# Linear attention and a gated FFN on one core: attention per whole batch on full 128x128 products, remainder tokens pooled in a ninth block, Gelu on ScalarE, loads cast on GpSimd, a fixed order

## The chip, the cores and the metric

One Trainium2 chip, one of its eight cores. The metric is the device time of one execution in microseconds; lower is better. Engines: TensorE (PE), VectorE (DVE), ScalarE (ACT), GpSimd (POOL) and SyncE (SP), the last only as a queue that issues DMAs. A tile lies in SBUF, or in PSUM, where TensorE writes its products.

## What is computed

Attention of a linear kind (softmax over the head dimension for q, over the tokens for k), whose output, laid out as tokens by channels, goes through a gated FFN. Eight batches, 8 heads, 576 tokens, 64 channels per head, all inputs float32.

```python
def _attn_ref(q, k, v):                          # (8, 8, 576, 64) each
    q_s = np.exp(q - max(q, axis=-1)); q_s = q_s / sum(q_s, axis=-1)
    k_s = np.exp(k - max(k, axis=2));  k_s = k_s / sum(k_s, axis=2)
    kv = np.einsum('bhsd,bhse->bhde', k_s, v)
    return np.einsum('bhsd,bhde->bhse', q_s, kv)

def _moe_ref(x, w_gate, w_val, w_out):           # x (4608, 512), weights 512x1536, 512x1536, 1536x512
    g = x @ w_gate
    gelu = 0.5 * g * (1.0 + erf(g / sqrt(2)))
    return (gelu * (x @ w_val)) @ w_out
```

Both kernels leave out the subtraction of the maxima, and divide kv by the column sums of exp(k), which a column of ones beside v provides.

## The kernel before

Two parts share the engines. **Attention** works on pairs of heads, 32 units (8 batches x 4 pairs). A pair's 1152 tokens lie on 128 partitions as nine chunks of 128, so chunk 4 holds the last 64 tokens of one head and the first 64 of the other. `attention_load` (lines 84 to 105) loads q and k by SP in runs of 256 B (one token's 64 floats) and v by a GpSimd DMA that casts to f16. `attention_main` (lines 107 to 168) takes exp on ACT, normalizes q on DVE (L115 sum, L117 reciprocal, L119 product), transposes q by ten TensorE products per pair (L128 to L137, copied to SBUF by ACT, L140 and L141), forms kv in ten small products (`pskv_a`, `pskv_b`, 65 columns, L145 to L153), and scales the two results into a block-diagonal 128x128 tile on DVE (L157 to L165). `attention_out` (lines 170 to 180) makes the pair's 128 channels of x for 576 tokens with two products (L174 of 512 columns, L176 of 64), cast by ACT into `xt_sb`, which holds x transposed for all 4608 tokens.

**The FFN** (`ffn_block`, lines 182 to 229) goes over nine blocks of 512 tokens, in order of token, so a block crosses batches. In each of 12 steps `fi` it forms 128 columns of gate (`psg`, four products, L191) and value (`psv`, L196), and the gated f16 tile `ht`: tanh on ACT (L200, Gelu as 0.5 g (1 + tanh)), then three passes on DVE (L204, L207, L210). Then four groups `psy` of 12 products each (L219) give 128 tokens of output; ACT scales them (L223) and SP stores them.

Before block 0 stand batch 0's attention, the loads of batch 1 and the issue of the gate and value weights (GpSimd DMAs that cast, 128 columns each). `ffn_block` then runs one attention stage (a load, a `main` or an `out` of batch blk+1 or blk+2) ahead of each `fi` step. The program's order is only the start: a scheduler at build time sets the order on each engine by its own costs, and pools of buffers (three of each attention tile, four PSUM banks for `psg`, `psv`, `psy` and `psxa`) limit how far it runs ahead.

Of the kernel before, what the change touches and what calls it, by code (L numbers as in the profile page):

```python
# [10 lines left out]
f16 = mybir.dt.float16  # L11

_TANH_C = 0.7978845608028654
# [4 lines left out]
def kernel(  # L18
# [13 lines left out]
    NTOK = B * S  # L32
# [3 lines left out]
    NCH = (2 * S) // P  # L36
    NCI = C // P
    NFI = F // P
    NBLK = 512
    NB = NTOK // NBLK  # L40
# [3 lines left out]
    xpool = ctx.enter_context(tc.tile_pool(name="xpool", bufs=1))  # L44
    att = ctx.enter_context(tc.tile_pool(name="att", bufs=3))
    ffn = ctx.enter_context(tc.tile_pool(name="ffn", bufs=3))
    htp = ctx.enter_context(tc.tile_pool(name="htp", bufs=24))
    ps_big = ctx.enter_context(tc.tile_pool(name="ps_big", bufs=4, space=bass.MemoryType.PSUM))
    ps_eqt = ctx.enter_context(tc.tile_pool(name="ps_eqt", bufs=2, space=bass.MemoryType.PSUM))
    ps_kv = ctx.enter_context(tc.tile_pool(name="ps_kv", bufs=2, space=bass.MemoryType.PSUM))  # L50

    def big_psum(name):
        return ps_big.tile([P, 512], f32, name=name, tag="mm")

    def small_psum(name):
        return ps_kv.tile([P, 72], f32, name=name, tag="kv")

    ident = const.tile([P, P], f16)
    make_identity(nc, ident)

    xt_sb = xpool.tile([P, H // 2, NTOK], f16)

    wtiles = {}

    def load_weights_gv():
        wg_sb = wpool.tile([P, NCI, F], f16, name="wg_sb")
        wv_sb = wpool.tile([P, NCI, F], f16, name="wv_sb")
        wg_src = moe_w_gate.rearrange("(ci p) f -> p ci f", p=P)
        wv_src = moe_w_val.rearrange("(ci p) f -> p ci f", p=P)
        for fi in range(NFI):  # L70
            sl = slice(fi * P, (fi + 1) * P)
            nc.gpsimd.dma_start(out=wg_sb[:, :, sl], in_=wg_src[:, :, sl])
            nc.gpsimd.dma_start(out=wv_sb[:, :, sl], in_=wv_src[:, :, sl])
        wtiles["g"] = wg_sb
        wtiles["v"] = wv_sb

    def load_weights_o():
        wo_sb = wpool.tile([P, NFI, C], f16, name="wo_sb")
        wo_src = moe_w_out.rearrange("(fi p) m -> p fi m", p=P)
        for fi in range(NFI):  # L80
            nc.gpsimd.dma_start(out=wo_sb[:, fi, :], in_=wo_src[:, fi, :])
        wtiles["o"] = wo_sb

    def attention_load(b: int, hp: int):
        h0 = 2 * hp
        qt = att.tile([P, NCH, D], f32)
        nc.sync.dma_start(
            out=qt,
            in_=q[b, h0:h0 + 2].rearrange("h s d -> (h s) d").rearrange(
                "(n p) d -> p n d", p=P),  # L90
        )
        kt = att.tile([P, NCH, D], f32)
        nc.sync.dma_start(
            out=kt,
            in_=k[b, h0:h0 + 2].rearrange("h s d -> (h s) d").rearrange(
                "(n p) d -> p n d", p=P),
        )
        vt = att.tile([P, NCH, 80], f16)
        nc.gpsimd.dma_start(  # L99
            out=vt[:, :, 0:D],  # L100
            in_=v[b, h0:h0 + 2].rearrange("h s d -> (h s) d").rearrange(
                "(n p) d -> p n d", p=P),
        )
        nc.vector.memset(vt[:, :, D:D + 1], 1.0)
        return qt, kt, vt

    def attention_main(b: int, hp: int, tiles):
        qt, kt, vt = tiles
        eq = att.tile([P, NCH, D], f16)
        nc.scalar.activation(out=eq, in_=qt, func=mybir.ActivationFunctionType.Exp)  # L110
        ek = att.tile([P, NCH, D], f16)
# [70 lines left out]
    def ffn_block(blk: int, interleave=()):  # L182
# [45 lines left out]
        for fn in inter:  # L228
            fn()
# [67 lines left out]
```

## Time and profile before

| | |
|---|---|
| median of 3 runs | 383.56 us (383.49 to 384.02) |
| the profiled execution, from first to last instruction | 381.9 us |
| PE busy | 350.7 us, 92% of the span, 2000 matmuls |
| DVE busy | 275.4 us, 72% |
| ACT busy | 187.6 us, 49% |
| POOL busy | 57.0 us, 15% |
| DMA | 38.10 MB, 131739 packets, of which 125568 under 512 B |
| mean granted TensorE clock | 0.973 of full speed |

The times are of unprofiled runs; the profile is one more execution, whose own time is known by its span. In the profile a group of instructions is a line of the kernel with its engine; in the groups the columns after the bar are the busy time in us, the mean of one in ns, then the engine's idle time just before them and what ended most of it. The chain of work that ended last lists start, length and work of each piece. The slices cut the span into 40 equal parts with the busy share in tenths.

### The profile page before, as it was taken

The page shows a single profiled execution, that of the slowest core. Times are in us where ns is not written, and L with a number is a line of the kernel's source. Part 1 is how long each engine was busy: PE and PEld are TensorE (multiplying, and loading weights), DVE is VectorE, ACT ScalarE, POOL GpSimd, SP SyncE. Part 2 cuts the span into 40 slices and gives each one's busy share as a digit, 9 for nine tenths or more (in the row PEclk, how much of TensorE's full clock was granted, in tenths as well). Part 3 has the DMA queues.
Part 4 walks back from the last instruction along what each step waited for, and adds up shares of the span by engine and source line. Part 5 has one row for each costly group of instructions (what it writes and reads, how often), then busy time and mean ns, then how long its engine had stood idle before and what let it go on. Part 6 is the DMA issues. An engine that isn't in the chain of part 4 may idle for free.

```text
span 381.9 us, 5586 instructions
## 1 busy us (share of the span) xinstructions
PE 350.7 (92%) x2000; PEld 167.7 (44%) x2000; DVE 275.4 (72%) x612; ACT 187.6 (49%) x337; POOL 57.0 (15%) x74
## 2 busy tenths in 40 slices
PE   2698582899999999999999999999999999999995
PEld 1444231345444544454445444545455444444442
DVE  3558275387986799679967987698568927954980
ACT  3764523537663757375737563657166313323321
POOL 5574444202010102010202020102010000000000
PEclk9999696699999999999999999999999999999999
DMA  9999999996685459546953883454130011011002
GB/s 164 202 194 169 168 173 184 194 237 112 100 94 145 74 78 124 146 66 88 120 149 65 120 94 100 71 65 31 66 62 2 0 67 45 0 46 66 0 1 110
DMA packets 131739, 38.10 MB, mean 100 GB/s; under 512 B 125568, under 2 KB 127104, under 8 KB 131712
## 3 DMA queue, kind: packets, MB, share of 16 engines
q1 hardware_dynamic: 79936, 28.32, 34.3%
q0 software_dynamic: 51776, 9.44, 29.8%
q8 instruction: 15, 0.25, 0.3%
q14 instruction: 12, 0.10, 0.1%
HBM read 37.75 MB, written 9.44 MB: 124 GB/s over the span
## 4 chain that ended last, share of the span: by engine, by line
PE 78%; DMA 14%; DVE 4%; ACT 2%; issue 1%; SPq 1%; ACTq 0%; DVEq 0%
PE psy L219 24%; PE psg L191 22%; PE psv L196 21%; DMA kt<-in_k_dram 9%; DMA qt<-in_q_dram 5%; PE pseqt_a L133 2%; PE pseqt_b L137 2%; DVE gv L207 2%; PE psxa L174 2%; PE pskv_b L153 1%; DVE gsc L204 1%; DVE ht L210 1%; PE pseqt_a L128 1%; PE pskv_a L147 1%; PE pskv_a L145 1%
## 5 line engine op out<-in xcount | busy, mean ns | idle before, releaser
L196 PE MATMUL psv<-xt_sb,wv_sb 128*128 128x512 f16 x432 | 113.3, 385 | 6.6 <-ACT xt_sb L179 5.7
L204 DVE TENSOR_SCALAR gsc<-psg 128x512 f32<-128x512 f32 x108 | 74.1, 687 | 62.5 <-ACT tnh L200 60.9
L191 PE MATMUL psg<-xt_sb,wg_sb 128*128 128x512 f16 x432 | 115.9, 389 | 0.0
L219 PE MATMUL psy<-wo_sb,ht 128*128 128x512 f16 x432 | 94.9, 379 | 0.2 <-DVE ht L210 0.2
L200 ACT ACTIVATE tnh<-psg 128x512 f32<-128x512 f32 x108 | 64.0, 594 | 58.8 <-PE psg L191 44.7
L207 DVE TENSOR_TENSOR gv<-gsc,psv 128x512 f32<-128x512 f32 x108 | 73.1, 678 | 4.0 <-PE psxb L176 1.6
L210 DVE SCALAR_TENSOR_TENSOR ht<-tnh,gv 128x512 f16<-128x512 f32 x108 | 73.3, 681 | 0.5
L196 PEld LDWEIGHTS <-wv_sb 128*128 128x128 f16 x432 | 42.7, 99 | 60.0 <-issue 10.0
L219 PEld LDWEIGHTS <-ht 128*128 128x128 f16 x432 | 41.9, 98 | 51.7 <-DVE ht L210 3.1
L99 POOL DMA_DIRECT2D vt<-in_v_dram x32 | 32.0, 1001 | 203.8 <-PE pskv_b L153 85.2
L191 PEld LDWEIGHTS <-wg_sb 128*128 128x128 f16 x432 | 38.5, 99 | 45.2 <-issue 3.9
L223 ACT ACTIVATE yo<-psy 128x512 f32<-128x512 f32 x36 | 21.5, 597 | 67.3 <-PE psy L219 67.3
L112 ACT ACTIVATE ek<-kt 128x576 f16<-128x576 f32 x32 | 21.9, 683 | 20.1 <-DMA kt<-in_k_dram 19.0
L110 ACT ACTIVATE eq<-qt 128x576 f16<-128x576 f32 x32 | 21.7, 679 | 18.4 <-DMA qt<-in_q_dram 9.4
L119 DVE TENSOR_TENSOR eqn<-eq,rrq 128x576 f16<-128x576 f16 x32 | 24.0, 750 | 5.8 <-PE pseqt_b L137 5.6
L140 ACT COPY eqt_sb<-pseqt_a 64x576 f16<-64x576 f16 x32 | 20.2, 630 | 14.9 <-PE pseqt_a L128 14.3
L115 DVE TENSOR_REDUCE rq<-eq 128x9 f32<-128x576 f16 x32 | 23.0, 722 | 6.0 <-ACT eq L110 5.9
L179 ACT CAST xt_sb<-psxa 128x512 f16<-128x512 f32 x32 | 18.7, 584 | 10.1 <-PE psxb L176 10.0
L174 PE MATMUL psxa<-eqt_sb,kv_sb 128*128 128x512 f16 x32 | 13.6, 426 | 10.1 <-ACT eqt_sb L141 8.8
L141 ACT COPY eqt_sb<-pseqt_b 64x576 f16<-64x576 f16 x32 | 20.2, 631 | 0.9
L133 PE MATMUL pseqt_a<-ident,eqn 128*64 128x128 f16 x128 | 15.1, 239 | 3.1 <-ACT eqt_sb L140 2.3
L145 PE MATMUL pskv_a<-vt,ek 128*64 128x65 f16 x128 | 10.3, 203 | 7.2 <-DMA vt<-in_v_dram 7.0
(35 smaller groups left out, 184.9 us busy)
## 6 DMA issues: line engine op xcount, KB each, us to landing
qt<-in_q_dram SPq DMA_DIRECT2D x32, 288.0 KB, 4.8
kt<-in_k_dram SPq DMA_DIRECT2D x32, 288.0 KB, 4.9
out_dram<-yo SPq DMA_DIRECT2D x36, 256.0 KB, 2.0
vt<-in_v_dram POOLq DMA_DIRECT2D x32, 144.0 KB, 5.1
wg_sb<-in_moe_w_gate_dram POOLq DMA_DIRECT2D x12, 128.0 KB, 12.1
wv_sb<-in_moe_w_val_dram POOLq DMA_DIRECT2D x12, 128.0 KB, 12.2
wo_sb<-in_moe_w_out_dram POOLq DMA_DIRECT2D x12, 128.0 KB, 9.2
```

Of the source, the lines that this page charges most:

```text
L99: nc.gpsimd.dma_start(out=vt[:, :, 0:D], in_=v[b, h0:h0 + 2].rearrange("h s d -> (h s) d").rearrange("(n p) d -> p n d", p=P),)
L112: nc.scalar.activation(out=ek, in_=kt, func=mybir.ActivationFunctionType.Exp)
L115: nc.vector.reduce_sum(rq, eq, axis=mybir.AxisListType.X)
L119: nc.vector.tensor_tensor(out=eqn, in0=eq, in1=rrq.unsqueeze(-1).to_broadcast((P, NCH, D)), op=mybir.AluOpType.mult,)
L133: nc.tensor.transpose(pseqt_a[0:64, j * P:(j + 1) * P], eqn[:, j, :], ident[:, :])
L191: nc.tensor.matmul(psg, wtiles["g"][:, ci, fi * P:(fi + 1) * P], xt_sb[:, ci, t0:t0 + NBLK], start=(ci == 0), stop=(ci == NCI - 1))
L196: nc.tensor.matmul(psv, wtiles["v"][:, ci, fi * P:(fi + 1) * P], xt_sb[:, ci, t0:t0 + NBLK], start=(ci == 0), stop=(ci == NCI - 1))
L200: nc.scalar.activation(out=tnh, in_=psg, func=mybir.ActivationFunctionType.Tanh, scale=_TANH_C)
L204: nc.vector.tensor_scalar(out=gsc, in0=psg, scalar1=0.5 * _H_SCALE, scalar2=None, op0=mybir.AluOpType.mult)
L207: nc.vector.tensor_tensor(out=gv, in0=gsc, in1=psv, op=mybir.AluOpType.mult)
L210: nc.vector.scalar_tensor_tensor(out=ht, in0=tnh, scalar=1.0, in1=gv, op0=mybir.AluOpType.add, op1=mybir.AluOpType.mult)
L219: nc.tensor.matmul(psy, hts[fi][:, ns * P:(ns + 1) * P], wtiles["o"][:, fi, :], start=(fi == 0), stop=(fi == NFI - 1))
```

## The change

The kernel is written anew around one batch at a time; the arithmetic of the FFN stays in products of 128x128 by 512 columns, nine blocks of 512 columns.

- **Blocks.** Of each batch's 576 tokens, 512 (on 128 partitions, four consecutive tokens each) are FFN block b. The other 64 of each batch are collected in `xtr` (8 x 64 = 512 columns), which is a ninth block at the end.
- **Attention.** A pair of heads is the 128 columns of one weight load. kv takes five products of 130 columns per pair (`unit_kv`, the fifth for the 64 remainder tokens, padded with zeros), whose off-diagonal halves a mask removes in the scaling. Transposes are full 128x128, four per pair and one for the remainder (`unit_t`, `unit_trem`). x is one product of 512 columns per pair (`unit_x`) and one of 64 (`unit_xrem`). The normalization of q runs on four heads at a time (`norm_sum`, `norm_mul`).
- **Engines.** Gelu is one ACT pass, and `ht` one DVE pass (value x 1024 x gelu). Transposed q is copied by DVE; x is copied by DVE up to batch 2 and by ACT from batch 3; DVE scales the output.
- **Loads.** All are plain float32 DMAs of SP: q, k and v in runs of 1 KB (remainder 256 B), weights in runs of 2 KB, 1 MB each, into eight shared staging buffers (`ldp`). GpSimd casts v and all weights to f16.
- **Order.** `manual_schedule` keeps each engine's instructions as written. Batch 1 and 2 get their norms and most of their attention behind the last output groups of blocks 0 and 1; batches 3 to 7 inside the steps of blocks 2 to 6.

Where things stand is read from the order of instructions on an engine. The first place is DVE at the passage from block 1 to block 2. Before (`rq`, `rrq`, `eqn`: norms of later pairs; `gsc`: the first pass of block 2's first step):

```order
L210 SCALAR_TENSOR_TENSOR ht_1857<-tnh_1851,gv_1855 128x512
L119 TENSOR_TENSOR eqn_2044<-eq_2036,rrq_2042 128x576
L161 MEMSET kv2_sb_2077 128x64
L115 TENSOR_REDUCE rq_2201<-eq_2197 128x9
L161 MEMSET kv2_sb_2238 128x64
L117 RECIPROCAL rrq_2203<-rq_2201 128x9
L115 TENSOR_REDUCE rq_2264<-eq_2260 128x9
L119 TENSOR_TENSOR eqn_2205<-eq_2197,rrq_2203 128x576
L117 RECIPROCAL rrq_2266<-rq_2264 128x9
```

Now (`yo`: scaled output of block 1; `rq`, `rrq`, `eq0`: norms of batch 2; `eqt`, `xt`: copies of its transposed q and of its x, which block 2's first products read):

```order
L159 TENSOR_REDUCE rq_879<-eq0_97 128x20
L163 RECIPROCAL rrq_881<-rq_879 128x20
L169 TENSOR_TENSOR eq0_97<-eq0_97,rrq_881 128x5x256
L267 TENSOR_SCALAR yo_877<-psy_884 128x512
L208 COPY eqt_899<-pst_900 128x2x512
L208 COPY eqt_899<-pst_910 128x2x512
L216 COPY eqt_899<-pstr_920 128x4x64
L229 CAST xt_926<-psx_927 128x512
L229 CAST xt_926<-psx_930 128x512
L229 CAST xt_926<-psx_933 128x512
L229 CAST xt_926<-psx_936 128x512
L253 SCALAR_TENSOR_TENSOR ht_969<-psv_962,gl_967 128x512
```

Before, DVE works there for later pairs, since block 2's x was finished inside block 1; now norms and copies of the very batch that block 2 reads stand between the blocks.

The second place is ACT between the same blocks. Before:

```order
L200 ACTIVATE tnh_1339<-psg_1329 128x512
L110 ACTIVATE eq_1973<-qt_1411 128x576
L223 ACTIVATE yo_1360<-psy_1347 128x512
L223 ACTIVATE yo_1376<-psy_1363 128x512
L110 ACTIVATE eq_2036<-qt_1436 128x576
L223 ACTIVATE yo_1392<-psy_1379 128x512
L223 ACTIVATE yo_1408<-psy_1395 128x512
L200 ACTIVATE tnh_1428<-psg_1418 128x512
```

Now (a table load, then the Exp of batch 2, `ek0` and `eq0`, and of batch 3, `ek1`):

```order
L251 ACTIVATE gl_779<-psg_769 128x512
L129 ACT_TABLE_LOAD
L129 ACTIVATE ek0_96<-kt_435 128x8x4x64
L136 ACTIVATE ek0_96<-kr_437 64x512
L129 ACTIVATE eq0_97<-qt_443 128x8x4x64
L136 ACTIVATE eq0_97<-qr_445 64x512
L129 ACTIVATE ek1_103<-kt_603 128x8x4x64
```

The Exp of a batch moved behind the last Gelu of a block, with a table load ahead; the first Gelu of the next block has another. The third place is SP's queue of loads at the start. Before, q and k of one pair alternate, while the weights stand in GpSimd's queue:

```order
L87 DMA qt_88<-in_q_dram 128x9x64
L93 DMA kt_90<-in_k_dram 128x9x64
L87 DMA qt_146<-in_q_dram 128x9x64
L93 DMA kt_148<-in_k_dram 128x9x64
L87 DMA qt_204<-in_q_dram 128x9x64
```

Now, behind batch 0's nine loads (`wgst`, `wvst`, `wost`: staged weights; `kt` to `qr`: batch 1):

```order
L109 DMA wgst_137<-in_moe_w_gate_dram 128x4x512
L109 DMA wvst_139<-in_moe_w_val_dram 128x4x512
L119 DMA wost_141<-in_moe_w_out_dram 128x4x512
L119 DMA wost_143<-in_moe_w_out_dram 128x4x512
L119 DMA wost_145<-in_moe_w_out_dram 128x4x512
L89 DMA kt_147<-in_k_dram 128x8x256
L95 DMA kr_149<-in_k_dram 64x8x64
L89 DMA vt_151<-in_v_dram 128x8x256
L95 DMA vr_153<-in_v_dram 64x8x64
L89 DMA qt_155<-in_q_dram 128x8x256
L95 DMA qr_157<-in_q_dram 64x8x64
```

The weights moved into the one queue that loads q, k and v, ahead of batch 1.

The diff, cut to the new functions and the loop that orders them:

```diff
+    ldp = ctx.enter_context(tc.tile_pool(name="ldp", bufs=8))
+    ps_big = ctx.enter_context(tc.tile_pool(name="ps_big", bufs=6, space=bass.MemoryType.PSUM))
+    ps_att = ctx.enter_context(tc.tile_pool(name="ps_att", bufs=2, space=bass.MemoryType.PSUM))
+    ctx.enter_context(tc.manual_schedule())
...
+    def load_main(src, nm, b, h0, h1):
...
+        nc.sync.dma_start(
+            out=tiles[key][:, h0:h1, :],
+            in_=src[b, h0:h1, 0:MAIN, :].rearrange("h (p n) d -> p h (n d)", n=NM))
...
+    def cast_w_gv(c):
+        sl = slice(c * WCH, (c + 1) * WCH)
+        nc.gpsimd.tensor_copy(out=wg_sb[:, :, sl], in_=wst[("wg", c)])
+        nc.gpsimd.tensor_copy(out=wv_sb[:, :, sl], in_=wst[("wv", c)])
...
+    def unit_kv(b, g):
+        pskv = ps_att.tile([P, 2, 2 * VW], f32, name="pskv", tag="att")
+        for j in range(2):
+            hp = 2 * g + j
+            for n in range(NM + 1):
+                nc.tensor.matmul(
+                    pskv[:, j, :], ek_b[b % 2][:, n, hp * P:(hp + 1) * P],
+                    v16_b[b % 2][:, n, 2 * hp:2 * hp + 2, 0:VW],
+                    start=(n == 0), stop=(n == NM))
...
+    def unit_t(b, g):
...
+        nc.vector.tensor_copy(out=eqt[:, 2 * g:2 * g + 2, 0:MAIN], in_=pst)
...
+        gl = ffn.tile([P, 512], f32, name="gl", tag="gl")
+        nc.scalar.activation(out=gl, in_=psg, func=ACTF.Gelu)
+        ht = htp.tile([P, 512], f16, name="ht", tag="ht")
+        nc.vector.scalar_tensor_tensor(
+            out=ht, in0=psv, scalar=_H_SCALE, in1=gl, op0=ALU.mult, op1=ALU.mult)
...
+    for b in range(B + 1):
+        xt = get_xt(b) if b < B else xtr
+        nb = b + 1
+        ahead = 2 <= b and nb < B
+        units = attention_units(nb) if ahead else [None] * NFI
+        norms = norm_units(nb) if ahead else []
+        if 1 <= b and b + 2 < B:
+            load_batch(b + 2)
+        hts = []
         for fi in range(NFI):
...
+            hts.append(ffn_fi(xt, fi))
+            if fi < len(norms):
+                norms[fi]()
+            if units[fi] is not None:
+                units[fi]()
+        if b == 0:
+            load_batch(2)
+            prepare(1)
+        elif b == 1:
+            prepare(2)
+            prepare(3)
+        elif b + 2 < B:
+            prepare(b + 2)
+        ffn_out(b, hts, 0)
+        if b <= 1:
+            nu, au = norm_units(nb), [f for f in attention_units(nb) if f is not None]
+            ffn_out(b, hts, 1)
+            for f in au[0:2] + nu[0:2]:
+                f()
+            ffn_out(b, hts, 2)
+            for f in nu[2:4]:
+                f()
+            ffn_out(b, hts, 3)
+            for f in au[2:]:
+                f()
```

`prepare(b)` is the four Exp passes of a batch and GpSimd's cast of its v. `attention_units` are, by step: kv of pairs 0 and 1, kv of 2 and 3, two empty steps, transposes of pairs 0 and 1, of 2 and 3, of the remainder, four `unit_x`, and `unit_xrem`.

More of the change, by code (lines that the diff above doesn't have):

```diff
@@ L31 @@
     B, H, S, D = q.shape
-    NTOK = B * S
     C = H * D
@@ L249, in mains_outs_of @@
[L249 to L266 removed]
+    mask = const.tile([P, 2, D], f32)
@@ new lines, with prepare @@
+    cast_v_rem(0)
+    norm_sum(0, 0, 4)
+    norm_mul(0, 0, 4)
+    unit_kv(0, 0)
+    unit_t(0, 0)
+    exp_main("k", 0, 4, 8)
+    exp_main("q", 0, 4, 8)
+    unit_x(0, 0)
+    unit_x(0, 1)
+    cast_v_main(0, 4, 8)
+    norm_sum(0, 4, 8)
+    norm_mul(0, 4, 8)
+    unit_kv(0, 1)
+    unit_t(0, 1)
+    unit_trem(0)
+    unit_x(0, 2)
+    unit_x(0, 3)
+    unit_xrem(0)
+    for c in range(3):
+        cast_w_gv(c)
+    for c in range(3):
+        cast_w_o(c)
+    def prepare(b):
+        exps(b)
+        cast_v_main(b, 0, H)
+        cast_v_rem(b)
```

407 lines of the change are left out of this document (207 added, 200 removed).

## Prediction

> **What bounds the kernel now.** I read the page first: the span, the slices, the groups.
>
> ```profile
> span 381.9 us, 5586 instructions
> PE   2698582899999999999999999999999999999995
> PEclk9999696699999999999999999999999999999999
> DMA  9999999996685459546953883454130011011002
> GB/s 164 202 194 169 168 173 184 194 237 112 100 94 145 74 78 124 146 66 88 120 149 65 120 94 100 71 65 31 66 62 2 0 67 45 0 46 66 0 1 110
> ```
>
> A slice is 9.5 us. From the ninth on TensorE is full, so nothing but less TensorE work can shorten that part. The first eight are another stage: DMA is at 9, yet moves only 164 to 202 GB/s, and TensorE is half empty at a lowered clock. Next I read the chain that ended last, for the places where an FFN block begins (first psg group of blocks 1, 2, 7 and 8, block 7's 48 psy products, and the last step).
>
> ```profile
> 85.79 0.86 PE psg L191 x4
> 124.36 0.86 PE psg L191 x4
> 315.89 0.86 PE psg L191 x4
> 336.61 10.36 PE psy L219 x48
> 346.97 0.86 PE psg L191 x4
> 378.13 0.60 ACT yo L223
> ```
>
> Five stages follow: 85.8 us until block 1 begins; block 1, 38.6; blocks 2 to 6, 191.5, or 38.3 each; blocks 7 and 8, 62.2, or 31.1 each; and 3.8 from the last psy to the end. Blocks 7 and 8 carry no attention: 144 matmuls of 512 columns at 0.216 us (10.36 for 48) are 31.1, the FFN's floor. So a block with attention pays 7.2 us for it. I work in these stages; the span is 381.9 and the median of the runs 1.7 above it, which I add at the end.
>
> **The first stage: loads.** It ends when the loads let it. I divide the time that packets took by their number. The rows are: the first 80 us, the packets of SP's queue from 86 to 280 us (21 stores of 128 packets of 2 KB, the rest 256 B loads), and the last 12 us (512 packets of 2 KB).
>
> ```profile
> DMA packets 58766, 14.36 MB, mean 179 GB/s; under 512 B 57225, under 2 KB 58761, under 8 KB 58761
> q1 hardware_dynamic: 42516, 15.48, 34.0%
> q1 hardware_dynamic: 576, 1.05, 23.3%
> ```
>
> The last gives 12 us x 16 engines x 0.233 / 512, some 85 ns for 2 KB. The middle one gives 1055 us less 2688 x 85 ns, over 39828 packets: 21 ns for 256 B. On a straight line, 1 KB takes 48 ns. The change loads q, k, v in 1 KB runs (64 remainder tokens per head in 256 B runs) and weights in 2 KB runs. Batch 0, the weights and batch 1 are 3.54 + 9.44 + 3.54 = 16.5 MB: 6144 packets of 1 KB, 4608 of 2 KB, 3072 of 256 B, together 752 us over 16 engines, or 47 us. With 3 us until the first lands, batch 0 is in at 14, the first gate chunk at 17, the last w_out at 39, batch 1's v at 46 and its q at 50. These are estimates: no row reads DRAM in long runs. One bound is the 2 KB stores' pace; the other is the 179 GB/s above, which is a rival below.
>
> Now what hangs on each landing. The rows are groups of operations of known size.
>
> ```profile
> L112 ACT ACTIVATE ek<-kt 128x576 f16<-128x576 f32 x32 | 21.9, 683 | 20.1 <-DMA kt<-in_k_dram 19.0
> L179 ACT CAST xt_sb<-psxa 128x512 f16<-128x512 f32 x32 | 18.7, 584 | 10.1 <-PE psxb L176 10.0
> L180 ACT CAST xt_sb<-psxb 128x64 f16<-128x64 f32 x32 | 7.0, 218 | 0.0
> L115 DVE TENSOR_REDUCE rq<-eq 128x9 f32<-128x576 f16 x32 | 23.0, 722 | 6.0 <-ACT eq L110 5.9
> L119 DVE TENSOR_TENSOR eqn<-eq,rrq 128x576 f16<-128x576 f16 x32 | 24.0, 750 | 5.8 <-PE pseqt_b L137 5.6
> L117 DVE RECIPROCAL rrq<-rq 128x9 f32<-128x9 f32 x32 | 6.5, 212 | 0.9 <-issue 0.7
> L210 DVE SCALAR_TENSOR_TENSOR ht<-tnh,gv 128x512 f16<-128x512 f32 x108 | 73.3, 681 | 0.5
> L162 DVE TENSOR_SCALAR kv_sb<-pskv_a,rck_a 64x64 f16<-64x64 f32 x32 | 8.4, 264 | 0.1
> L110 ACT ACT_TABLE_LOAD x1 | 1.3, 1283 | 0.7 <-PEq L281 0.7
> masks.py:199 POOL TENSOR_SCALAR_AFFINE_SELECT ident<-ident 128x128 f16<-128x128 f16 x1 | 0.3, 304 | 0.1
> masks.py:197 POOL MEMSET ident<- 128x128 f16 x1 | 0.2, 205 | 0.3 <-POOLq L281 0.3
> ```
>
> And two DVE operations of the chain, the second waiting for the first (start, length): 0.10 us lie between them.
>
> ```profile
> 296.35 0.61 DVE gsc L204
> 297.06 0.70 DVE gv L207
> ```
>
> ACT: 366 ns for 448 elements more is 0.82 ns each, so 2048 elements take 1.85 us, 512 take 0.6, and a batch's four Exp 4.9. DVE: about 1.04 ns an element over some 0.13. Half a batch's norm (1280 elements) is a sum of 1.46, a reciprocal of 20 at 0.30 and a multiply of 1.48: 3.25, and 6.5 for both. A copy of 1024 transposed elements takes 1.27, of 256 takes 0.4, an xt copy 0.68 like ht; a kv unit 0.8 (two products of 128 from 0.264 for 64, and a reciprocal).
>
> GpSimd's cast of 2048 elements is unknown. At the memset's pace (205 ns, over about 95 fixed, for 128) it is 1.85 us; at the select's, which reads and writes, 3.4. I take 3.3, the nearer kind. Nine casts from 17 on end at 47, and v of batch 1 with its remainder at 51. Casts this slow just feed block 0, whose twelve steps need 20.7 us: it begins at 24, when the first value chunk is cast, and ends its steps near 46, a cold clock included. Two psy groups follow until 51.5, then batch 1's kv (needs v, 51) until 53.4; DVE has finished kv at 55. q's Exp is done by 53, so DVE's order sets the rest: 55, norms 6.5, two yo 1.4, transposed copies 2.9, four xt copies 2.7. That is 68.5, where the last of them starts block 1. Eight dependent operations at 0.10 us of hand-over add 0.8, and three of four matmuls need no last xt, so 0.6 comes off. TensorE has nearly idled before it, and a first group then runs cold:
>
> ```profile
> 23.49 1.71 PE psg L191 x4
> 72.77 1.80 PE psg L191 x4
> 74.57 0.86 PE psv L196 x4
> ```
>
> 0.86 us become 1.7 to 1.8, for one to two groups: up to 1.7 us lost, where a warm clock would lose none. I take 1.3. Block 1 begins at **70.0** instead of 85.8. SP's own queue adds nothing here: batch 1's k, v and q reuse the staging of value chunk 0 and of chunk 1, cast by 31, before SP comes to them at 39; batch 2's loads, ahead of block 0's stores, wait last for the first w_out cast (41).
>
> **Block 1** has no attention inside its steps, but batch 2's behind it. Its steps end at 90.7. ACT must then load the Exp table (1.28) behind the last Gelu (0.7, an ACT pass of 512 and a hand-over), and run four Exp (4.9): 97.6. Then DVE does the same chain: norms 6.5, two yo 1.4, copies 2.9 and 2.7, hand-overs less overlap 0.2: 111.3. With 1.3 for the clock block 2 begins at 112.6: **42.6** instead of 38.6, and TensorE, done with its psy and kv at 103, waits. Batch 3's Exp queue behind batch 2's on ACT and end by 103; Gelu comes later, so they cost nothing. [...] In later blocks two loads of 1.28, four Exp and a Gelu are 8.2 us of ACT beside 10.4 us of psy.
>
> **Blocks 2 to 6** hold the attention inside. The chain shows today's pieces at a warm clock:
>
> ```profile
> 278.74 0.24 PE pskv_b L153 x4
> 282.16 0.97 PE psg L191 x4
> 283.99 0.22 PE psxa L174
> 284.21 0.03 PE psxb L176
> 287.94 0.34 PE pseqt_a L133 x4
> 288.76 0.12 PE pskv_a L145 x4
> ```
>
> Today a batch takes 40 transposes, 40 kv products and 8 output products. It becomes 20 transposes of the same 128 columns at 0.085, or 1.7; 20 kv products of 130 columns, not shown: 0.03 to 0.06 for 65, so 0.06 to 0.12, I take 0.08: 1.6; 4 x 0.25, or 1.0; and 0.11 lost by the group behind each of five units of small weights (0.97 against 0.86): 0.55. That is 4.9 (4.4 to 5.7). DVE has 9.2 us of norms and ht and 1.6 of kv in the first four steps, where TensorE takes 8.2; three pairs of psum absorb most of it, and I take 0.5 of waiting for the second transpose unit. So 31.1 + 4.9 + 0.5 is 36.5, and five are **182.5** instead of 191.5. The removed DVE products (three of 0.68 a step become one) give nothing more, since 1.73 us of TensorE a step was cover for most of them. The remainder block is 128 x 512 like the others, so nine blocks stay nine: 62.2 and 3.8 hold, with yo now DVE's (0.68).
>
> Sum: 70.0 + 42.6 + 182.5 + 62.2 + 3.8 = 361.1, and 1.7 to the median: **363**.
>
> **Rivals.** *The loads stay slow* (slower than before): long runs don't raise the rate, because DRAM reads and not packets limit it. For it speaks that every read-bound slice lies near 180 GB/s; against it that these slices hold 57225 packets under 512 B of 58766. At 179 GB/s the 16.5 MB land at 95 instead of 50; the Exp and DVE chain behind q (17 us) begins block 1 at 112, and the time is 405. It turns slower than before where q lands after 73, below some 235 GB/s. Chance 0.05.
>
> *GpSimd casts slowly*: block 1's start follows 10.25 casts. At 5 us each, half again the select's pace, it is 17 us later: 380. Beyond 5.3 it is slower than before. 0.12, of which 0.01 lies there.
>
> *The steady blocks don't shrink*: DVE's norms stand before ht in its order, and a longer wait gives back the 9 us saved: 372. Against it: DVE has 22 us of work in 36. 0.10.
>
> *Better than summed*: casts at the memset's pace, a clock that holds, kv at 0.06 and no DVE wait: block 1 would begin at 66 (then q's landing leads) and last 41, a later block 35.5: 352. 0.12.
>
> My forecast, 356 to 370 by the bounds above, keeps 0.61. With the better case, the unshrunk blocks and the near part of the slow casts, **350 to 376** leaves out under 0.2. A measurement here tells about 0.2% from no change. Faster by more: 0.93 (all but the slow loads and the far end of the casts); within: 0.01; slower: 0.06.
>
> **What would show it.** Right: block 1 begins near 70, with DVE busy and TensorE idle for some 8 us before blocks 1 and 2 alone; blocks 2 to 6 at 36.5; the last batch 1 load landing near 50; casts near 3.3 us. Wrong: loads below 235 GB/s, casts of 5 us, TensorE waiting for ht in each steady block, or a lowered clock behind the ninth slice.

## The result, and the profile after

| | before | after |
|---|---|---|
| time, median of 4 runs each (range) | 383.52 us (383.11 to 384.02) | 351.62 us (350.89 to 353.71) |
| span of the profiled execution | 381.9 us | 351.8 us (that execution took 353.71) |
| until block 1 begins | 85.8 | 70.9 |
| block 1 | 38.6 | 40.9 |
| blocks 2 to 6 | 191.5 | 173.1 |
| blocks 7 and 8 | 62.2 | 62.2 |
| after the last psy | 3.8 | 4.7 |

The ratio is 0.917, with a 95% interval of 0.914 to 0.920: 8.3% faster. The time lies in the range of the prediction, 1.6 us above its lower end and 4 us below its forecast's own 356 to 370. The stages above are read as before, from where the first psg group of each block begins; the timelines of TensorE show the same starts 0.2 us sooner than the chain. First the slices of the page after (8.8 us each):

```profile
PE   0259999499987999999999999999999999999994
PEclk9999999789996999999999999999999999999999
DMA  7999999893016900296039404940300020011013
GB/s 192 330 388 386 344 278 284 241 269 94 3 60 188 270 6 2 96 276 153 0 117 287 120 2 135 277 112 0 121 1 0 8 113 0 2 60 60 2 30 89
```

DMA stands at 9 as before, but now for seven slices at up to 388 GB/s. These rates are not of one kind: what GpSimd's casting queue moved before is counted by the f16 bytes written, half of what was read (its 9.44 MB in the page before stand for 18.87 MB of weights and v, without which the page's 37.75 MB read from HBM do not come out). In the first 80 us before, that queue moved 6.34 MB and SP's 7.96 with one store of 0.26, so some 255 GB/s were read, and not 179. Behind the start TensorE has just two dips, in the eighth slice and the thirteenth: ahead of blocks 1 and 2, where it is idle for 5.0 and 3.3 us. The chain that ended last (start, length, work) has the beginnings of blocks 0 to 4, with the groups behind the first one, and the norms ahead of block 1:

```profile
26.69 1.71 PE psg L244 x4
28.40 1.71 PE psv L248 x4
30.11 1.56 PE psg L244 x4
...
58.89 1.49 DVE eq L169
...
62.72 3.20 DVE eq L169
70.89 1.65 PE psg L244 x4
...
111.78 1.68 PE psg L244 x4
...
147.08 0.86 PE psg L244 x4
...
181.54 0.86 PE psg L244 x4
```

Block 2 takes 35.3 us (111.78 to 147.08) with a slow first group, and each later one 34.46. In a first group of 1.65 to 1.71 a product of 512 columns takes some 0.43 us instead of 0.216; I call that cold. Only blocks 0, 1 and 2 have one. The granted clock was 0.56 in that of block 1 (70.89 to 72.54) and 0.54 in that of block 2 (111.78 to 113.46). In block 0's slow groups it reads 1.00, as it does in the kernel before at 23.5 us, so that there only the equal pace speaks for the clock, and the cause isn't shown. The other thing to see is the multiply of the norms, `eq L169`: it takes 1.49, and once 3.20.

The groups by form show what the casts and copies cost:

```profile
L114 POOL CAST wg_sb<-wgst 128x2048 f16<-128x2048 f32 x3 | 5.7, 1891 | 2.9 <-DMA wgst<-in_moe_w_gate_dram 2.9
...
L208 DVE COPY eqt<-pst 128x1024 f16<-128x1024 f16 x16 | 10.8, 682 | 0.9 <-PE pst L205 0.9
```

A GpSimd cast of 2048 elements takes 1.89 us, nearly the memset's pace, and not the 3.3 taken; it waits for its DMA. Only one weight cast, of a value chunk, took 3.10. A copy of 1024 transposed f16 elements takes 0.68, not 1.27.

The passage from block 1 to block 2, from the timelines of ACT and DVE (start, length, operation):

```profile
91.57 0.60 ACT L251 ACTIVATE gl<-psg 128x512 f32<-128x512 f32 x1 [1.13 <-PE psg L244]
92.19 1.28 ACT L129 ACT_TABLE_LOAD   x1
93.48 1.91 ACT L129 ACTIVATE ek<-kt 128x2048 f16<-128x2048 f32 x1
...
97.62 0.61 ACT L136 ACTIVATE eq<-qr 64x512 f16<-64x512 f32 x1
```

```profile
98.22 0.16 DVE L185 RECIPROCAL rck<-pskv 128x2 f32<-128x2 f32 x1
...
99.66 1.48 DVE L159 TENSOR_REDUCE rq<-eq 128x20 f32<-128x1280 f16 x1
...
107.33 1.30 DVE L208 COPY eqt<-pst 128x1024 f16<-128x1024 f16 x2
...
109.30 2.65 DVE L229 CAST xt<-psx 128x512 f16<-128x512 f32 x4 [0.33 <-PE psx L226]
```

The last Exp ends at 98.2, but the norms begin at 99.7, behind the first two yo and the kv units in DVE's order. From there DVE works on without waiting for ACT or a load (0.33 for the first psx is its longest wait) until the last xt copy ends at 111.95; block 2 begins just before, as its first matmuls don't need that copy.

In the steady blocks the chain (block 4 here) has the attention's pieces between the groups:

```profile
183.26 0.58 PE pskv L180 x10
...
191.32 0.45 PE pst L205 x8
...
193.49 0.58 PE pst L205 x8
...
195.80 0.22 PE pstr L214 x4
...
197.75 0.21 PE psx L226
...
205.52 0.12 PE psxr L236 x4
```

Eight transposes take 0.45, 0.056 each; the second eight take 0.13 more: they start at 193.46, when the second multiply of the norms has ended at 193.40, so this is a wait. Twenty transposes (1.12), twenty kv products (1.15), four psx (0.85), psxr (0.12) and that wait are 3.37 us, which is what the block has over 31.08.

### The profile page after: what moved, and what is told of

It reads as the page before. It is cut to its first block, busy times and chain, and to the rows that moved or that the text cites. A ratio compares the mean times of both kernels' runs of the same rounds, so it can differ in the third digit from the quotient of the medians.

```text
span 351.8 us, 4287 instructions
## 1 busy us (share of the span) xinstructions
PE 319.6 (91%) x1680; PEld 152.8 (43%) x1680; DVE 179.9 (51%) x283; ACT 135.7 (39%) x184; POOL 42.4 (12%) x36
## 3 DMA queue, kind: packets, MB, share of 16 engines
HBM read 37.75 MB, written 9.44 MB: 134 GB/s over the span
## 4 chain that ended last, share of the span: by engine, by line
PE 85%; DVE 10%; DMA 2%; issue 1%; SPq 1%; ACT 0%
PE psg L244 27%; PE psv L248 27%; PE psy L262 24%; DVE eq L169 3%; DVE rq L159 2%; PE psx L226 2%; DMA qt<-in_q_dram 2%; PE pst L205 2%; PE pskv L180 2%; DVE xt L229 1%; DVE yo L267 1%; DVE eqt L208 1%; DVE kv_sb L188 1%; PE pstr L214 1%; DVE rrq L163 0%
## 5 line engine op out<-in xcount | busy, mean ns | idle before, releaser
L253 DVE SCALAR_TENSOR_TENSOR ht<-psv,gl 128x512 f16<-128x512 f32 x108 | 74.1, 686 | 92.1 <-PE psv L248 91.5
L251 ACT ACTIVATE gl<-psg 128x512 f32<-128x512 f32 x108 | 64.5, 597 | 144.7 <-PE psg L244 136.1
L244 PE MATMUL psg<-xt,wg_sb 128*128 128x512 f16 x384 | 101.8, 389 | 0.0
L248 PE MATMUL psv<-xt,wv_sb 128*128 128x512 f16 x384 | 99.5, 382 | 0.0
L248 PEld LDWEIGHTS <-wv_sb 128*128 128x128 f16 x432 | 42.6, 99 | 52.5 <-issue 2.7
L244 PEld LDWEIGHTS <-wg_sb 128*128 128x128 f16 x432 | 41.6, 99 | 46.0 <-issue 2.8
L267 DVE TENSOR_SCALAR yo<-psy 128x512 f32<-128x512 f32 x36 | 24.8, 690 | 60.7 <-PE psy L262 60.7
L147 POOL CAST v<-vt 128x2048 f16<-128x2048 f32 (+1 forms) x9 | 16.4, 1824 | 179.7 <-DMA vt<-in_v_dram 166.6
L159 DVE TENSOR_REDUCE rq<-eq 128x20 f32<-128x1280 f16 x16 | 23.6, 1476 | 9.6 <-ACT eq L136 9.6
L169 DVE TENSOR_TENSOR eq<-eq,rrq 128x1280 f16<-128x1280 f16 x16 | 25.4, 1590 | 0.2
L205 PE MATMUL pst<-ident,eq 128*128 128x128 f16 x128 | 11.5, 242 | 14.5 <-DVE rck L185 7.8
L129 ACT ACTIVATE eq<-qt 128x2048 f16<-128x2048 f32 (+1 forms) x9 | 15.4, 1709 | 6.4 <-DMA qt<-in_q_dram 6.4
L205 PEld LDWEIGHTS <-eq 128*128 128x128 f16 x128 | 9.0, 108 | 19.3 <-DVE eq L169 9.3
L129 ACT ACTIVATE ek<-kt 128x2048 f16<-128x2048 f32 (+1 forms) x9 | 15.5, 1719 | 3.6 <-DMA kt<-in_k_dram 3.5
```

What stands on the lines that cost most here:

```text
L129: nc.scalar.activation(out=dst[:, 0:NM, h0 * D:h1 * D].rearrange("p n (h d) -> p h n d", d=D), in_=tiles[(nm, b)][:, h0:h1, :].rearrange(" ...
L159: nc.vector.reduce_sum(rq, eq_b[b % 2][:, :, h0 * D:h1 * D].rearrange("p n (h d) -> p n h d", d=D), axis=mybir.AxisListType.X)
L169: nc.vector.tensor_tensor(out=e, in0=e, in1=rr[(b, h0)].unsqueeze(-1).to_broadcast((P, NM + 1, n, D)), op=ALU.mult)
L205: nc.tensor.transpose(pst[:, j, n * P:(n + 1) * P], eq_b[b % 2][:, n, hp * P:(hp + 1) * P], ident)
L244: nc.tensor.matmul(psg, wg_sb[:, ci, fi * P:(fi + 1) * P], xt[:, ci, :], start=(ci == 0), stop=(ci == HP - 1))
L248: nc.tensor.matmul(psv, wv_sb[:, ci, fi * P:(fi + 1) * P], xt[:, ci, :], start=(ci == 0), stop=(ci == HP - 1))
```

## The experiments

Theory: the gain of the start is the loads' run length and their single queue; blocks 1 and 2 wait for DVE's serial chain (norms, copies) between blocks; a steady block is FFN plus the attention's own TensorE time, which is smaller than predicted because transposes with 128 weight columns are faster (0.056 us) than the row that priced them (0.085). Rivals: that other parts (Gelu on ScalarE, the fixed order, the casts) carry the gain; that DVE's removed passes matter; that GpSimd's cast of v disturbs the norms.

**Tanh again, with its DVE passes.** One Gelu becomes what it was before; everything else stays.

```diff
-        nc.scalar.activation(out=gl, in_=psg, func=ACTF.Gelu)
+        nc.scalar.activation(out=gl, in_=psg, func=ACTF.Tanh, scale=0.7978845608028654)
+        nc.vector.tensor_scalar(out=gsc, in0=psg, scalar1=0.5 * _H_SCALE, scalar2=None, op0=ALU.mult)
+        nc.vector.tensor_tensor(out=gsc, in0=gsc, in1=psv, op=ALU.mult)
...
-            out=ht, in0=psv, scalar=_H_SCALE, in1=gl, op0=ALU.mult, op1=ALU.mult)
+            out=ht, in0=gl, scalar=1.0, in1=gsc, op0=ALU.add, op1=ALU.mult)
```

> The changed kernel with the old gating: tanh on ScalarE (Gelu as 0.5 g (1 + tanh), so no table switches) and three DVE passes a step instead of one; all else as changed. The prediction said that the two removed passes give nothing more: then within 2 us of the changed kernel's 351.6, and less the table loads. Rival: they are what lets the attention fit beside the steps. DVE is busy 19.4 us of a 34.5 us block; 24 passes at 0.6 make it 33.8, and in the first four steps it would have 15 us of work beside 8.1 us of TensorE. Then blocks 2 to 6 take 36.5 to 38.5 each instead of 34.46, and the time is 361 to 371.

Measured: 428.8 us (427.1 to 433.0), 1.119 of before [1.112, 1.126], and a steady block of 44.2 us. That is outside both the theory and the rival. Its DVE timeline in a steady block:

```profile
197.64 0.68 DVE L253 TENSOR_SCALAR gsc<-psg 128x512 f32<-128x512 f32 x1
...
199.76 0.69 DVE L253 TENSOR_SCALAR gsc<-psg 128x512 f32<-128x512 f32 x1
```

The period is 2.12 us, three dependent passes with their hand-overs, against TensorE's 1.73 for a step. Its windows over the steps of a steady block and over the psy behind them (length; busy time of PE, PEld, DVE, ACT, POOL; clock; DMA share; GB/s):

```profile
214.20:248.10 33.90, 28.47 (x155) 13.78 (x153) 31.17 (x49) 11.11 (x18) 2.45 (x2) 0.90 0.44 121
248.10:258.50 10.40, 8.76 (x42) 3.77 (x41) 4.26 (x7) 3.42 (x4) 0.00 (x0) 1.00 0.13 52
```

The twelve steps take 33.9 us with DVE nearly full and TensorE waiting for it; in the 10.4 of psy DVE is busy for 4.26 only. In this fixed order the removed passes are worth 77 us, and not nothing.

**The same, with the framework's scheduler ordering the instructions,** to see whether that is the passes or the order.

```diff
-    ctx.enter_context(tc.manual_schedule())
```

> The changed kernel with tanh and three DVE passes, and without the fixed order. With the fixed order that gating took 428.8 us, a step of three passes that wait for each other taking 2.12 us of DVE. Theory: it is the order as much as the passes: a scheduler that puts another step's pass between them brings a step to 1.8 us, as before the change; DVE then has 34 us of work in a block, and the time is 365 to 385. Rival: the amount of DVE work alone did it, and the time stays over 410.

Measured: 360.3 us (356.7 to 360.5), 0.937 [0.933, 0.941], below the 365 to 385 expected. Blocks 3 to 6 take 34.3 to 34.5 us, as with Gelu. The windows over psy of one block and the steps of the next:

```profile
178.30:188.60 10.30, 10.30 (x49) 4.66 (x48) 10.30 (x15) 0.35 (x1) 0.00 (x0) 1.00 0.13 52
188.60:212.60 24.00, 24.00 (x146) 12.15 (x144) 23.93 (x44) 13.96 (x20) 2.91 (x2) 1.00 0.06 23
```

DVE is busy all of the time and TensorE still never waits: the scheduler lays the norms beside psy and lets ht run late. Two ht of successive steps in its timeline:

```profile
178.68 0.68 DVE L256 SCALAR_TENSOR_TENSOR ht<-gl,gsc 128x512 f16<-128x512 f32 x1
...
180.48 0.68 DVE L256 SCALAR_TENSOR_TENSOR ht<-gl,gsc 128x512 f16<-128x512 f32 x1
```

A step's passes come every 1.80 us here, since passes of other steps stand between those that depend on each other. That is 0.32 less than in the fixed order, 3.8 for twelve steps; and DVE has no idle time beside psy, where the fixed order left it 6.1. The two add up to 9.9 us, as much as the fixed order's block is longer (44.2 against 34.3). The passes then cost only in block 0 (54.6 us against 50.2 in the next experiment) and in blocks 1 and 2 (40.7 and 38.0 against 39.1 and 35.7). So the prediction's "give nothing more" holds in steady blocks for an order that fills psy with norms, and fails for the one that the changed kernel has.

**The scheduler with Gelu.** The changed kernel without its fixed order, the same one line.

> The changed kernel without the fixed order: the scheduler at build time orders each engine's work again. Theory: the order as written is no gain in blocks 2 to 6, which stand at TensorE's floor (31.1 + 3.36), so 34.5 each also here, and the two passages behind blocks 0 and 1, where TensorE idles for 7.9 us, could only get shorter: 342 to 352. Rival: the scheduler moves loads, casts or norms so that block 0 or the steps wait: over 356.

Measured: 353.5 us (351.9 to 354.5), 0.921 [0.918, 0.924], against 351.6 and, run again beside others, 352.5 for the fixed order: between the theory (342 to 352) and the rival (over 356). Block 0 begins sooner, at 20.8, but with two products only; its transposes and x products come between, and the rest follows from 26.1. It ends its steps 2 us sooner, and then waits 6.3 us for the norms of batch 1, so that it takes 50.2 us instead of 44.2 and block 1 begins at 71.0, where it began at 70.7. By itself the fixed order gains nothing that these runs can tell.

**Loads in short runs.** The four chunks of each q, k and v load come from 128 consecutive tokens again, 256 B a run; weights and queue are untouched. The store of the output is adapted.

```diff
-        nc.sync.dma_start(
-            out=tiles[key][:, h0:h1, :],
-            in_=src[b, h0:h1, 0:MAIN, :].rearrange("h (p n) d -> p h (n d)", n=NM))
+        for n in range(NM):
+            nc.sync.dma_start(
+                out=tiles[key][:, h0:h1, n * D:(n + 1) * D],
+                in_=src[b, h0:h1, n * P:(n + 1) * P, :].rearrange("h p d -> p h d"))
```

> The changed kernel with q, k and v loaded in 256 B runs again (partition p holds tokens p, 128 + p, ..., four DMAs per load; stores in 2 KB runs instead of 4 KB). Theory: the length of the runs sets when batch 1 is in. 24576 packets at 21 ns take the place of 6144 at 42.5 ns (1 KB at 385 GB/s), so q of batch 1 lands (24576 x 21 - 6144 x 42.5) / 16 = 16 us later, block 1 begins near 86 instead of 70.9, and the time is 366 to 369. Rival: the gain came from leaving out the casting queue; then under 3 us.

Measured: 362.3 us (359.7 to 362.6), 0.942 [0.938, 0.946], some 10 us slower than the change, where some 15 were expected. The DMA view of its first 80 us, in slices of 2 us:

```profile
GB/s 10 206 194 215 193 189 194 200 227 214 359 328 372 400 394 390 387 386 388 385 386 383 277 108 237 186 216 217 194 217 214 202 217 209 207 221 150 228 230 265
```

Batch 0 at about 200 GB/s, the weights in 2 KB runs mostly at 383 to 400, batch 1 at about 210. The run length sets the rate, as both sides of the estimate have it; the price is 2 us ahead of block 0 (28.8 against 26.5), 4 to 5 more in front of block 1 (77.4 against 70.7), and the rest in blocks 1 and 2 (41.9 and 36.8 instead of 40.9 and 35.3).

**Weights cast by the DMA.** GpSimd's queue loads them straight into f16, as before the change, with no staging and no GpSimd casts.

```diff
-            t = ldp.tile([P, HP, WCH], f32, name=f"{nm}st", tag="ld")
-            nc.sync.dma_start(out=t, in_=w.rearrange("(ci p) f -> p ci f", p=P)[:, :, sl])
+            nc.gpsimd.dma_start(out=(wg_sb if nm == "wg" else wv_sb)[:, :, sl],
+                                in_=w.rearrange("(ci p) f -> p ci f", p=P)[:, :, sl])
```

> The changed kernel with the weights loaded by casting DMAs of GpSimd's queue again, in the same 2 KB source runs (1 MB each, no staging, no GpSimd cast). Theory: only the run length of the reads matters: the weights are in at about the same time and the time is within 2 us of 351.6. Rival: casting DMAs are slow in themselves. In the first 80 us before, GpSimd's queue took 82.1% of 16 engines for 6.34 MB, 6 GB/s an engine or 97 GB/s for 16; 9.4 MB would take 97 us, block 0's output could not end before 100, and the time would be 380 to 395.

Measured: 367.6 us (366.7 to 368.1), 0.958 [0.956, 0.960]. The time lies between the theory (within 2 us) and the rival (380 to 395). Nearly all of the 15 to 16 us more lie ahead of block 0, which begins at 41.4 instead of 26.5. Its chain begins:

```profile
13.33 20.11 DMA qt<-in_q_dram
...
41.55 1.71 PE psg L239 x4
```

and that of the change:

```profile
3.35 7.63 DMA qt<-in_q_dram
```

The weights start at once in their own queue and share the 16 engines with batch 0, whose last half of q takes 20.1 us to land. The DMA view of the first 60 us, in slices of 1.5 us:

```profile
GB/s 0 147 300 266 218 201 221 238 234 218 210 221 237 245 246 245 248 246 246 246 247 247 248 247 241 227 207 240 343 332 211 319 279 220 309 277 227 291 281 239
...
q0 software_dynamic: 4752, 4.72, 46.3%
```

While both queues run, the view has 201 to 248 GB/s, against 386 for plain loads in one queue. But GpSimd's queue (q0) counts f16 bytes again: its 4.72 MB are the 9.44 MB of the weights. From 4 to 34 us SP's queue moved 3.45 MB and GpSimd's 3.63, so 10.7 MB were read, or 357 GB/s. So the plain loads are worth more than the run length of q, k and v, and little of that is left for the rate: most is the one queue, which puts batch 0 first. An edit that changes only one of the two wasn't run.

**The change again,** unaltered, beside the next three.

> The changed kernel again, unaltered, as the measure for the kernels run beside it: 350.9 to 353.7, stages of 70.9, 40.9, 173.1, 62.2 and 4.7 us.

Measured: 352.5 us (351.6 to 355.6), 0.919 [0.916, 0.922]. The slow multiply is gone here, and GpSimd's cast of v, which begins 0.28 us behind the multiply, is slow in its place (from the two engines' timelines):

```profile
61.45 1.49 DVE L169 TENSOR_TENSOR eq<-eq,rrq 128x1280 f16<-128x1280 f16 x1
61.73 2.98 POOL L147 CAST v<-vt 128x2048 f16<-128x2048 f32 x1 [10.45 <-DMA vt<-in_v_dram]
```

In the first run the cast began 0.04 us ahead of the multiply that took 3.20, and took its usual time:

```profile
62.68 1.89 POOL L147 CAST v<-vt 128x2048 f16<-128x2048 f32 x1 [10.56 <-DMA vt<-in_v_dram]
```

So the one that begins first takes its usual time, and the other ends late by nearly what it needs alone: in the first run the multiply 1.35 us after the cast's end (65.92 against 64.57), in this one the cast 1.77 after the multiply's (64.71 against 62.94). They do not run side by side. The other overlaps in these traces show the same, such as the 3.10 of the value chunk's cast, which began 0.14 us behind a multiply.

**The steady order from block 1 on.** Batch 2's attention is put inside block 1 as it is in later blocks (its x is then copied by ACT, in lines not shown), so only block 1 is preceded by the serial passage.

```diff
-        ahead = 2 <= b and nb < B
+        ahead = 1 <= b and nb < B
...
             prepare(1)
-        elif b == 1:
             prepare(2)
-            prepare(3)
...
-        if b <= 1:
+        if b == 0:
             nu, au = norm_units(nb), [f for f in attention_units(nb) if f is not None]
```

> Batch 2's attention moved inside the steps of block 1, as it is for batches 3 to 7: its Exp and cast follow batch 1's behind block 0's steps, its x is copied by ACT. Theory: the wait before block 2 is the serial chain Exp, norms, copies and goes away: block 1 takes 34.5 to 35.5 instead of 40.9, and the time is 345 to 346.5. Rival: batch 2's q lands so late (its DMA is issued at 57, with 10 us to landing) that ACT, whose queue holds block 1's Gelu behind those Exp, starts block 1 late by 2 to 5 us: 347 to 350.

Measured: 346.6 us (345.0 to 346.9), 0.902 [0.900, 0.904], 5.9 us faster than the change beside it. Its chain, where block 1 ends:

```profile
95.13 10.36 PE psy L262 x48
105.49 0.86 PE psg L244 x4
```

All of psy runs through, and the first group of block 2 is warm. Block 1 takes 36.7 us where the change takes 40.9 and 41.5, block 2 34.5 instead of 35.3 and 35.6. That is the serial passage behind block 1 with its cold clock, shown by its removal.

**v of batch 2 loaded last** (k, q, v), so that GpSimd's cast of it falls behind the norms. With the multiply at its usual 1.49 in place of 3.20, block 1 was to begin at 69.2 instead of 70.9, and the time to fall by 1.7 us.

```diff
-        for src, nm in ((k, "k"), (v, "v"), (q, "q")):
+        order = ((k, "k"), (q, "q"), (v, "v")) if b == 2 else ((k, "k"), (v, "v"), (q, "q"))
+        for src, nm in order:
```

> Only the loads of batch 2 in the order k, q, v instead of k, v, q. [...]

Measured: 353.3 us (352.8 to 353.5), 0.920 [0.918, 0.922]. The cast now begins at 65.47 and takes its 1.90, and the multiply its 1.49, but the time is that of the change. The passage from psy to block 1 takes 21.1 us in the first run of the change, 19.4 in the second and 19.4 here: the collision cost 1.7 in the first run and nothing in the second, where the cast came second, and no gain in the time is shown.

**Both together.**

> Both edits together: batch 2's attention inside block 1, and batch 2's loads in the order k, q, v, which also brings its q in earlier. Theory: the two gains add: block 1 begins near 69.2 and takes 34.5 to 35.5, 343 to 345. [...]

Measured: 346.5 us (345.5 to 346.8), 0.902 [0.900, 0.904]: with the steady order from block 1 on the fastest version here, and not to be told from it; the two gains that were expected to add (343 to 345) don't.

**Each of the 16 main transposes done twice,** to the same place, to price one.

```diff
             for n in range(NM):
                 nc.tensor.transpose(
                     pst[:, j, n * P:(n + 1) * P],
                     eq_b[b % 2][:, n, hp * P:(hp + 1) * P], ident)
+            for n in range(NM):
+                nc.tensor.transpose(
+                    pst[:, j, n * P:(n + 1) * P],
+                    eq_b[b % 2][:, n, hp * P:(hp + 1) * P], ident)
```

> The changed kernel with each of the 16 main transposes of a batch done twice into the same place (128-column weights, 128 columns moved). Theory: a transpose with 128-column weights costs its streaming time, 0.056 us as in the chain after (0.45 us for 8 behind another product), so a block of 2 to 6 is 16 x 0.056 = 0.9 us longer than 34.46. Rival: weight loads of 128 columns, back to back without a long product to hide them, show at 0.085 or more, 1.4 us a block and more.

**The added ones on 64 weight columns instead of 128.** The second transpose overwrites what they leave.

```diff
+            for n in range(NM):
+                nc.tensor.transpose(
+                    pst[0:64, j, n * P:(n + 1) * P],
+                    eq_b[b % 2][:, n, hp * P:hp * P + 64], ident)
```

> The same, but the first of each pair transposes only 64 columns of channels (64-column weights, 128 columns moved, output in the upper 64 partitions), as the kernel before did. Theory: the products before cost 0.085 us since weights of 64 columns load slowly: 16 x 0.085 = 1.36 us a block more than 34.46, that is 0.46 us more than with the full ones. Rival: the width of the weights makes no difference, and the price before came from its surroundings: 0.9 us, as with the full ones.

Measured: 357.0 us (356.3 to 358.5), 0.930 [0.927, 0.932], with full ones added; 366.3 us (365.7 to 368.4), 0.956 [0.953, 0.959], with narrow ones. A steady block rises from 34.46 to 35.22 and to 36.12. The chains, full ones first, then the narrow (L205) and the full ones (L209) in turn:

```profile
193.81 0.22 PE pst L205 x4
194.03 0.22 PE pst L209 x4
```

```profile
199.25 0.34 PE pst L205 x4
199.59 0.33 PE pst L209 x4
...
205.39 0.22 PE pstr L218 x4
```

A transpose on 128 weight columns takes 0.055 us, on 64 it takes 0.085, as in the kernel before, though it computes half as much. Sixteen full ones are 0.89, of which 0.13 went into the wait that was there before: 0.76 more a block. The full ones that follow the narrow ones take 0.083 too, and the four of the remainder, which stand alone, 0.055; why the neighbours slow down is open. So within this run the two widths cost the same; that the narrow ones are the cause rests on the run with full ones alone, and on the row of the kernel before. The group of weight loads in the profile before (PEld) says what the prediction's row for a transpose was:

```profile
L133 PEld LDWEIGHTS <-eqn 128*64 128x64 f16 x128 | 9.0, 117 | 16.9 <-issue 11.4 <-DVE vt L104 1.6 <-DVE eqn L119 1.5
```

64 columns. From 125 to 310 us such a load took 108 ns there, and one of 128 columns 98: half as many columns took 10 ns longer, a third of the 30 by which the transposes differ. What makes up the rest isn't shown.

**Batch 1 ahead of w_out.** The last serial passage is taken apart too: batch 1 is loaded before the w_out chunks, in the order k, q, v, its Exp stand behind step 7 of block 0, its norms behind steps 8 to 11, and its kv, transposes and x between block 0's psy groups.

```diff
+    load_batch(1)
     for c in range(3):
         load_w_o(c)
-    load_batch(1)
...
+            if b == 0 and fi == 7:
+                exps(1)
+            if b == 0 and fi >= 8:
+                norm_units(1)[fi - 8]()
```

> A faster version, built on batch 2's attention inside block 1. Batch 1 is loaded ahead of w_out; its Exp follow Gelu 7 of block 0, its norms the steps 8 to 11, and its kv, transposes and x stand between block 0's psy groups. Theory: the wait before block 1 is the loads' order and DVE's serial chain, and both go behind psy: block 1 begins near 65.5 instead of 70.9, and the time is 339 to 342. Rival: w_out lands too late (near 52 instead of 43) or ACT's Exp hold up Gelu 8, so block 0 loses what the passage gains: 345 to 348.

Measured: 348.0 us (347.2 to 349.8), 0.907 [0.905, 0.910], as the rival had it, and slower than the version that only moves batch 2's attention into block 1. Its timelines of ACT and then TensorE, in block 0:

```profile
40.15 0.60 ACT L252 ACTIVATE gl<-psg 128x512 f32<-128x512 f32 x1 [1.13 <-PE psg L245]
40.77 1.28 ACT L130 ACT_TABLE_LOAD   x1
...
48.12 1.57 ACT L252 ACTIVATE gl<-psg 128x512 f32<-128x512 f32 x3
```

```profile
48.77 1.87 PE L245 MATMUL psg<-xt,wg_sb 128*128 128x512 f16 x4 [2.61 <-ACT gl L252]
...
58.16 0.70 PE L206 MATMUL pst<-ident,eq 128*128 128x128 f16 x8 [1.73 <-DVE kv_sb L189]
```

Between the Gelu that ends at 40.75 and the next at 48.12 lie 7.4 us of Exp and two table loads on ACT. TensorE runs out of free psum, waits 2.61, and is cold again when it resumes (its first group takes 1.87 in this timeline, where the one ahead of the wait took 1.03); behind that DVE's norms make it wait 1.73 for kv_sb. Block 0 takes 44.4 us, where it took 41.9 with the passage left in place and only batch 2's attention moved: new waits took the place of the old one.

## Why the prediction was right or wrong

The sum of the stages was 361.1 and the span is 351.8. The 9.3 us are +0.9 at the start, −1.7 in block 1, −9.4 in blocks 2 to 6, none in blocks 7 and 8, +0.9 at the end. To the sum I added 1.7, the median's distance from the span before; here the median lies 0.2 below the span, since the profiled execution was 2.1 slower than it.

**The loads: right, but 2 to 4 us late.** q of batch 1 was expected at 50; its Exp begins at 54.0, after a wait of 0.65 for it. The last w_out cast begins at 41.6 (39 expected for the landing), v's at 49.7 (46), each after a wait for its DMA. Plain 2 KB runs read at 381 to 391 GB/s. "The loads stay slow" is excluded. Its price was also too high: the 179 GB/s counts half of what the casting queue reads. At the 255 that were read the 16.5 MB land near 68 and not 95, and the time would be near 378 and not 405, so that this rival was a loss of the gain and not a slower kernel.

**70.0 against 70.9: right by errors that cancel.** Casts take 1.89 and not 3.3, so they do not set the start of block 0. It begins at 26.7 and not at 24: batch 0's own chain of Exp, norms, transposes and copies does that, from the arrival of q at 11. With cold groups that cost 2.4 (1.71, 1.71 and 1.56 in place of 0.86) and not 1.3, DVE's order behind psy starts the norms at 57.1 and not at 55: +2.1. The stretched multiply added 1.7. The copies of transposes took 1.3 less, the 1.3 for the clock of block 1 falls behind its start, and hand-overs were 0.3 shorter. Together +0.9.

**Block 1, 40.9 against 42.6: mechanism right.** DVE's serial chain between the blocks sets it, as the run that removes it shows with 5.9 us. Its terms: the cold group in the steps +0.8; ACT done 1.1 sooner, as the last Gelu ends before TensorE's last group does; the norms 1.4 later than the Exp allows, behind kv, which the sum had as finished; copies and hand-overs −1.6; and the 1.3 for the clock of block 2, which again falls behind its start. The table load stands between the last Gelu and the first Exp with no gap of note: it starts 0.02 after the Gelu's end, and its own end, 93.47, is the Exp's start but for 0.01. So this switch cost the 1.28 of the load, as the sum had it.

**Blocks 2 to 6, 173.1 against 182.5: the step that failed is the size of the attention's TensorE time,** "That is 4.9 (4.4 to 5.7)" and the 0.5 of waiting. Measured are 3.24 and 0.13. "20 transposes of the same 128 columns at 0.085" were not the same: the row's weights had 64 columns. That is 0.6 us a block. kv at 0.058 and not 0.08 is 0.45, the 0.55 for groups behind small weights isn't there, as the psg and psv groups stand at 0.86, and 0.37 is the wait; the output products were right (0.97 for 1.0). That is 2.0 us less, five times, with 0.85 given back by the cold first group of block 2.

**The removed DVE products "give nothing more": wrong for this order,** and right for a better one in the steady blocks only. The statement took DVE's busy time against TensorE's. What counts in a fixed order is that the three passes of a step depend on each other (2.12 us a step instead of 1.80), and that with the norms standing among them the steps need more than TensorE takes, while DVE idles beside psy.

**The rivals.** "Better than summed" named 352, and the time is 352, by casts at the memset's pace, kv at 0.06 and nearly no wait; but a clock that holds and a block 1 at 66 were not part of it. That its number is met is luck: the start came 4.9 us later than it had and blocks 2 to 6 were 4.4 shorter. Slow casts and unshrunk blocks are excluded by the casts' 1.89 and the 34.46. One sign of being wrong did show, a lowered clock behind the ninth slice (the 6 in the thirteenth); but the sum itself had put 1.3 us for a cold group there, so the sign contradicted the sum and tells nothing against it.

**Blocks 7 and 8 and the end.** 62.2 is as forecast; the end takes 0.9 more. The last block's rows go out as eight DMAs of 64 tokens a piece, which may be why; that wasn't tried:

```profile
340.06 8.87 SPq L278 DMA_DIRECT2D out_dram<-yo  x8
```

## What to carry to other kernels

Before taking an instruction's price from a row, compare all of its shape with the new one, the weights' columns too: a half as wide one cost half again as much here (0.085 us against 0.055). In an order written by hand, add up the dependent passes of one step, not an engine's busy share; ask what an operation that is put in front of them holds up, and what the engine has left to do while TensorE is busy elsewhere. Before comparing the rates of two DMA queues, ask whether their bytes are counted before or behind a cast. When a serial passage between blocks is all that is left, hide it behind work of the same kind where its inputs are early; brought forward to where the engines are in use, it makes a new wait.

## What the hardware showed that was not expected

- GpSimd's f32 to f16 cast of 128x2048 took 1.89 us, 0.9 ns an element. Beside a DVE multiply of two SBUF operands the one that began second waited for the first: a multiply of 1.49 took 3.20 or 2.18 and ended 1.35 after the cast, a cast took 2.98 or 3.10 and ended some 1.75 after the multiply.
- One queue of plain loads in 2 KB runs read DRAM at 381 to 391 GB/s (slices of 1 us, from 18 to 38 us); with casting DMAs in GpSimd's queue beside it the two read some 357 GB/s together, which the profile shows as 236, since it counts a casting DMA by the f16 bytes written.
- DVE copied 1024 f16 elements from PSUM in 0.68 us, where 512 elements from f32 take the same.
- A transpose took 0.055 us with 128 weight columns and 0.085 with 64, and full ones behind narrow ones took 0.083.
